# q, k and f loaded without their last 16 rows, half of the first f issued by ScalarE, GpSimd's first copy of chunk ends put behind the first pair's products

## The chip, the core and the metric

The kernel runs on one core of a Trainium2 chip. A core has five engines with an instruction queue each: TensorE (PE in the profile, with its weight loads as PEld), VectorE (DVE), ScalarE (ACT), GpSimd (POOL) and SyncE (SP), and 16 DMA engines that all DMA issues share. The metric is the device time of one execution in microseconds (us), the median over several runs. Before the change it is 168.49 us, the median of 3 runs (167.91 to 168.71).

## The reference

A gated linear attention over 4 batches, 8 heads, 768 tokens and a head dimension of 48 is followed by a soft mixture of 8 experts with 4 slots each.

```python
f = 1.0 / (1.0 + np.exp(-f_logit))
for t in range(S):
    state = f[:, :, t, :, None] * state + np.einsum('bhd,bhe->bhde', k[:, :, t], v[:, :, t])
    y[:, :, t] = np.einsum('bhd,bhde->bhe', q[:, :, t], state)
...
logits = x @ phi
# d: softmax of logits over tokens, c: softmax over slots
slot_input = (d.T @ x).reshape(E, S_per_e, D)
for e in range(E):
    slot_out[e] = np.maximum(slot_input[e] @ w1[e], 0.0) @ w2[e]
return c @ slot_out
```

Everything is float32: x is 3072 x 384, w1 is 8 x 384 x 1024, w2 is 8 x 1024 x 384.

## The kernel before

**Tiling.** Two heads of a batch make a pair; there are 16 pairs, four to a batch. A pair's q, k and f lie in SBUF as 128 rows by 768 tokens: head 0 in rows 0 to 47, head 1 in rows 64 to 111, and filling rows between and behind them. The host writes these filling rows into the arrays too (line 1091), so each of these loads carries 128 rows (384 KB). What computes on them uses the first PW = 112 rows. The tokens fall into six chunks of 128.

**A pair's work** (the function attention). ScalarE takes exp(-f) (decay_exp, line 330) and ln(1 + that) (line 334). VectorE sums this along each chunk by a scan (Lb, line 338). ScalarE turns the sums into two factors, gb and pb (lines 341, 344). k is multiplied by gb and q by pb (line 347), on VectorE for pair 0 and, mostly, on GpSimd later. TensorE transposes k (kt, line 367), forms the scores of each half (sc, line 379), which VectorE masks (scb, line 384), the sums kv (line 413), and the output y from scores (line 404) and from the states (line 427). The states come from a scan of VectorE (line 417) that needs pbx, the factors at the chunk ends spread out by a copy of GpSimd (decay_pbx, line 361; helper line 321). Then y is copied (yT), gives its logits (line 459) and is transposed into x (line 438).

**Pair 0** is worked in two halves of 384 tokens, HALVES, so that the first scores come early: its f and q are loaded as halves (load_half), and its products are done half by half on VectorE.

**What sets the order.** A planner (class Plan) takes every operation with a due time and a cost per engine, and writes one list. The queues of the compute engines follow the due times. DMA issues on SyncE's queue are placed by the planner's account of the DMA engines: an issue of kb kilobytes takes kb / RATE us there (RATE = 385), and issues may run AHEAD of it by 2.3 us. The expert weights (w1 in pieces of 384 KB, line 564, then w2, line 568) are pushed into the room that this account leaves between the loads of q, k, f and v. Each weight load also waits for a step of computation ("pace", line 1014), and each DMA issue waits for the one eight before it, whose semaphore it takes. keep_order (line 45) then fixes every engine's own order.

**The start.** ScalarE's first work is the load of its activation table (line 229). SyncE's first issues are the two halves of f, k, the first half of q, the f of pair 1, and the second half of q. GpSimd copies pair 0's pbx as soon as ScalarE has written the second half of pb.

**A second way through** (general, line 1061) is taken only where the factors leave a safe range; a branch skips it, and it doesn't run here.

Of the kernel before, what the change touches and what calls it, by code (L numbers as in the profile page):

```python
# [14 lines left out]
B, H, S, D = 4, 8, 768, 48  # L15
# [6 lines left out]
NP = B * H // 2  # L22
PPB = H // 2
PW = 112
# [33 lines left out]
def flat(t):  # L58
    n = len(t.shape)
    if n == 2:  # L60
        return t
    names = "abcde"[: n - 1]
    return t.rearrange(f"p {' '.join(names)} -> p ({' '.join(names)})")
# [9 lines left out]
class Plan:  # L73
# [22 lines left out]
    def op(self, name, engs, fn, *args, r=(), w=(), x=(), due=0.0, take=(), free=(), kb=0, home=False, ni=0):  # L96

        name, mode = name if isinstance(name, tuple) else (name, None)
        deps = set()
        for key in r:  # L100
            if key in self.writer:
                deps.add(self.writer[key])
        for key in (*w, *x):
            if key in self.writer:
                deps.add(self.writer[key])
            deps.update(self.readers.get(key, ()))
        fixed = self.fixed and "SP" not in engs
        o = Op(len(self.ops), name, engs, fn, args, due, deps, take, free, kb, home, ni, mode, fixed)
        self.ops.append(o)
        for key in w:  # L110
            self.writer[key] = o
            self.readers[key] = []
        for key in r:
            self.readers.setdefault(key, []).append(o)
        for key in (*r, *w):
            self.uses.setdefault(key, []).append(o)
        return o
# [91 lines left out]
N_F, N_L, N_G, N_P, N_K, N_Q, N_V, N_SC, N_KT, N_S, N_Y = 3, 2, 2, 2, 3, 3, 4, 2, 2, 2, 3  # L209
# [4 lines left out]
def gla_soft_moe_kernel(ctx: ExitStack, tc: tile.TileContext, q, k, f, v, vt, phi, w1, w2, out):  # L214
# [7 lines left out]
    nc = tc.nc  # L222
# [3 lines left out]
    def P(shape, name, dt=F32):  # L226
        return pool.tile(shape, dt, tag=name, name=name)

    nc.scalar.preload_act_table_set("natural_log_exp_and_others")

    tc.mark_branch_hint_location("general", engines=list(nc.engines))
    plan = Plan(dict(a=3, b=2))
# [2 lines left out]
    def unit(key):  # L235
        u = plan.unit_of[key]
        un[key] = ps.tile([128, 1024 if u[0] == "a" else 512], F32, tag=u, name=str(key[0]), bufs=1)
        return un[key]


    fb = [P([128, S], f"fb{i}") for i in range(N_F)]
    Lb = [P([128, S], f"Lb{i}") for i in range(N_L)]

    starts = P([128, NM, C], "starts")
# [3 lines left out]
    kb = [P([128, S], f"kb{i}") for i in range(N_K)]  # L248
    qb = [P([128, S], f"qb{i}") for i in range(N_Q)]
# [5 lines left out]
    pbx = [P([128, D, NM], f"pbx{i}") for i in range(N_S)]  # L255
# [67 lines left out]

    def load(o, dst, src):
        nc.sync.dma_start(dst, src)


    def decay_exp(o, i, cs, n):
# [393 lines left out]
    op = plan.op  # L722
# [12 lines left out]
    HALVES = (slice(0, S // 2), slice(S // 2, S))  # L735
# [14 lines left out]
        START[name, i] = -80 + n  # L750
    START["e", 1], START["ln", 1], START["L", 1], START["dq", 2] = -95, -92, -94, 8.5

    def load_half(o, dst, src, cs):
        nc.sync.dma_start(dst[:, cs], src[:, cs])

    def attention(i):

        z = i * T
        F_, L_, G, PB, K, Q = (
            [(name, i % n, h) for h in range(2)]  # L760
            for name, n in (("fb", N_F), ("Lb", N_L), ("gb", N_G), ("pb", N_P), ("kb", N_K), ("qb", N_Q))
        )
# [4 lines left out]
        KK, S0, S1, YY, KV, XT, PL = ("kt", i), ("sc", i, 0), ("sc", i, 1), ("y", i), ("kv", i), ("xt", i), ("pl", b)  # L767

        if i == 0:
            for h, cs in enumerate(HALVES):  # L770
                op("lf", {"SP": 0.45}, load_half, fb[0], f[0], cs, w=F_[h : h + 1], due=-99, kb=192)
        else:
            op("lf", {"SP": 0.45}, load, fb[i % N_F], f[i], w=F_, due=z - (25 if i > 1 else 18.5), kb=384)
        op("lk", {"SP": 0.45}, load, kb[i % N_K], k[i], w=K, due=z - 14, kb=384)
        if i == 0:

            for h, cs in enumerate(HALVES):
                op("lq", {"SP": 0.45}, load_half, qb[0], q[0], cs, w=Q[h : h + 1], due=-12 + 0.7 * h, kb=192)
        else:
            op("lq", {"SP": 0.45}, load, qb[i % N_Q], q[i], w=Q, due=z - 12, kb=384)  # L780
        op("lv", {"SP": 0.45}, load, flat(vb[i % N_V]), v[i], w=[V], due=z - (6 if i else 11.2), kb=288)

        def gates(cs, hs, due, n, es):
# [85 lines left out]
    for b in range(B):  # L869
        for i in range(PPB * b, PPB * b + PPB):  # L870
            first_op.append(len(plan.ops))
            attention(i)
            past_op.append(len(plan.ops))
        batch_from.append(len(plan.ops))
        if b < L:
            mixture(b, (PPB * b + PPB) * T)
# [27 lines left out]
    n, asked = 0, set()  # L904
# [10 lines left out]
    z = NP * T + 4  # L915
# [6 lines left out]
    y = (NP - 1) * T  # L922
# [48 lines left out]
    for part in range(len(PARTS)):  # L971
# [9 lines left out]
        for shared in range(2):  # L981
# [5 lines left out]
            for x in range(4 * shared, 4 + 2 * shared):  # L987
# [3 lines left out]
                n = 1 if part == 2 else 2  # L991
# [5 lines left out]
    def emit(o):  # L997
        o.fn(o, *o.args)
# [4 lines left out]
    for o in order:  # L1003
        if o.name == "so2" and o.args == (1,):
            bad = nc.values_load(gbad[:1, :1], min_val=0, max_val=1)
        n0 = len(list(written))
        emit(o)
        new = list(nc.cur_bb.bb.instructions)[n0:]
        if o.name in ("lw1", "lw2"):

            before = [(d.end, n, d) for n, d in enumerate(steps) if d.end < o.begin - plan.LAT]
            if before:
                tc.add_manual_dep(
                    new[-1], last_of[max(before)[2].n], mybir.DependencyInfo(mybir.DependencyClass.Sync, mybir.DependencyReason.DATA),
                    reason="pace",
                )
        elif o.eng != "SP":
            steps.append(o)
            last_of[o.n] = new[-1].name
# [8 lines left out]
    NE4 = 12  # L1028

    def general_pair(i):  # L1030

        kq, qt = kb[0], qb[0]
        u, ft = (w1a[:, NE4 * S * x : NE4 * S * (x + 1)].rearrange("p (e t) -> p e t", e=NE4) for x in range(2))

        nc.sync.dma_start(ft, f[i].unsqueeze(1).broadcast_to([128, NE4, S]))
        nc.sync.dma_start(kq, k[i])
        nc.sync.dma_start(qt, q[i])
        nc.scalar.activation(ft[:PW], ft[:PW], AF.Exp, scale=-1.0)
        nc.gpsimd.tensor_scalar(ft[:PW], ft[:PW], 1.0, 3.0e38, op0=ALU.add, op1=ALU.min)
        nc.vector.reciprocal(ft[:PW], ft[:PW])  # L1040

        nc.vector.memset(ft[:PW, :, 0:1], 0.0)
        py = unit(("y", i))
        for n in range(D // NE4):
            nc.sync.dma_start(flat(u), vt[i, :, NE4 * n : NE4 * n + NE4].rearrange("r e t -> r (e t)").unsqueeze(1).broadcast_to([2, 64, NE4 * S]))
            nc.gpsimd.tensor_tensor(u[:PW], u[:PW], kq[:PW].unsqueeze(1).broadcast_to([PW, NE4, S]), op=ALU.mult)
            nc.vector.tensor_tensor_scan(flat(u)[:PW], flat(ft)[:PW], flat(u)[:PW], 0.0, op0=ALU.mult, op1=ALU.add)
            nc.gpsimd.tensor_tensor(u[:PW], u[:PW], qt[:PW].unsqueeze(1).broadcast_to([PW, NE4, S]), op=ALU.mult)
            for e in range(NE4):

                c = D - 1 - (NE4 * n + e)
                for x in range(2):
                    at = c + 256 * (1 - x)
                    nc.tensor.matmul(
                        py[:PW, 512 * x : 512 * x + 384], sel[:PW, at : at + PW], u[:PW, e, 384 * x : 384 * x + 384],
                        start=n == 0 and e == 0, stop=n == D // NE4 - 1 and e == NE4 - 1,
                    )
        for o in by_pair[i]:
            emit(o)
# [25 lines left out]
def _layout(inputs):  # L1085
    import numpy as np

    a = {}

    for n, name, fill in (("q", "q", 0.0), ("k", "k", 0.0), ("f", "f_logit", 30.0)):  # L1090
        y = np.full((NP, 2, 64, S), fill, np.float32)
        y[:, :, :D] = inputs[name].reshape(NP, 2, S, D).transpose(0, 1, 3, 2)
        a[n] = y.reshape(NP, 128, S)
    a["v"] = inputs["v"].reshape(NP, 2, NM, C, D).transpose(0, 3, 2, 1, 4).reshape(NP, C, NM * 2 * D)
    a["vt"] = inputs["v"].reshape(NP, 2, S, D).transpose(0, 1, 3, 2)
    ph = np.zeros((2, 64, 2, PPB, NS), np.float32)
    for x in range(2):
        ph[:, :D, x] = inputs["moe_phi"].reshape(PPB, 2, D, NS).transpose(1, 2, 0, 3)[:: -1 if x else 1]
    a["phi"] = ph.reshape(128, 2, PPB, NS)[:PW]
    a["w1"] = inputs["moe_w1"].reshape(NE, 3, 128, F).transpose(0, 2, 1, 3).reshape(NE, 128, 3 * F)  # L1100
    w2 = inputs["moe_w2"].reshape(NE, 8, 128, DM).transpose(0, 2, 1, 3)
    a["w2"] = np.concatenate([w2[..., c].reshape(NE, 128, -1) for c in PARTS], axis=2)
    return {n: np.ascontiguousarray(x, dtype=np.float32) for n, x in a.items()}
# [34 lines left out]
```

## Time and profile before

| | |
|---|---|
| median of 3 runs | 168.49 us |
| the profiled execution | 168.29 us |
| its span, first to last instruction | 166.6 us |
| mean granted TensorE clock | 0.984 |
| moved by DMA | 54.05 MB, read 48.87 MB |
| DMA queue of SyncE | 86.2% of 16 engines' span |
| loads of k, f, q | 16, 15 and 15 of 384 KB, and two halves each of the first f and q |
| median us from issue to landing of these | 7.4, 7.3, 7.3 |

The span lies 1.7 us under the execution's time; these lie around it. In the page, rows of 40 digits cut the span into slices of 4.2 us, where 9 is a slice that was busy for 90% or more. A row of the timeline reads: start, duration, engine, line, operation, out<-in, partitions x elements, count, and in brackets the idle time of that engine just before and what ended it. SPq and ACTq are issues of DMAs by SyncE and ScalarE; their duration is that of the issue, not of the transfer. A row of the chain gives start, duration, engine and line of the work that the end waited for. A row of a stretch gives its bounds and length, then busy time and count for PE, PEld, DVE, ACT and POOL, the granted clock, the share of the DMA engines and GB/s.

### The profile page before, as it was taken

Reading aid. Unit: us, or ns where it says so; the run is one execution under the profiler, and the core shown is the slowest. Engines: PE = TensorE matmul, PEld = TensorE weight load, DVE = VectorE, ACT = ScalarE, POOL = GpSimd, SP = SyncE. Lnnn points to the kernel's source line nnn. Section 1 sums busy time; section 2 is a strip of 40 time slices with the busy share of each in tenths; the row PEclk is TensorE's granted clock in tenths of the full one; section 3 lists DMA queues with packets and bytes.
Section 4 is the critical chain, followed back from the end, with each engine's and each line's share of the span. In section 5 each row is a group of like instructions: output and inputs, shape, how many; then the busy total and the mean of one; then the engine's idle time right before and its main releaser. Section 6 shows DMA issues by size and latency. Waiting matters only on the chain.

```text
span 166.6 us, 6386 instructions
## 1 busy us (share of the span) xinstructions
PE 153.7 (92%) x2724; PEld 123.3 (74%) x2724; DVE 116.6 (70%) x167; ACT 94.2 (57%) x166; POOL 89.9 (54%) x87
## 2 busy tenths in 40 slices
PE   5999999999999999999998999999899999999800
PEld 2367879889998969889896889988655449788700
DVE  4899999989979876898996989838432216043330
ACT  5899597967977949678783872631521121232310
POOL 5108969889889886897997889660000001000000
PEclk9999999999999999999999999999999999999985
DMA  5999999999999999999997559999999792055784
GB/s 134 320 407 370 390 399 398 399 398 393 395 393 397 397 397 399 396 398 398 398 377 248 182 173 293 340 363 407 398 398 389 233 360 85 6 215 211 281 295 151
DMA packets 20609, 54.05 MB, mean 325 GB/s; under 512 B 2288, under 2 KB 2912, under 8 KB 20576
## 3 DMA queue, kind: packets, MB, share of 16 engines
q1 hardware_dynamic: 20432, 53.34, 86.2%
q8 instruction: 22, 0.36, 0.9%
q10 hardware_dynamic: 144, 0.26, 0.4%
q14 instruction: 11, 0.09, 0.1%
HBM read 48.87 MB, written 4.72 MB: 322 GB/s over the span
## 4 chain that ended last, share of the span: by engine, by line
PE 67%; DVE 14%; POOL 5%; issue 4%; DMA 3%; ACT 3%; SPq 1%; POOLq 0%; ACTq 0%; DVEq 0%
PE sc L379 10%; PE y L404 9%; PE po L670 7%; PE up L625 7%; PE y L427 6%; PE kv L413 5%; PE kt L367 5%; DVE Lb L338 5%; PE xt L438 4%; PE pl L459 3%; PE pf L712 3%; DMA kb<-in_k_dram 3%; DVE scb L384 3%; POOL ce L545 2%; PE pi L502 2%
## 5 line engine op out<-in xcount | busy, mean ns | idle before, releaser
L347 POOL TENSOR_TENSOR kb<-kb,gb 112x768 f32<-112x768 f32 x15 | 27.4, 1830 | 16.3 <-ACT gb L341 12.8
L338 DVE TENSOR_TENSOR_SCAN Lb<-starts,fb 112x768 f32<-112x768 f32 (+1 forms) x17 | 35.1, 2063 | 1.6 <-ACT fb L334 1.6
L384 DVE TENSOR_TENSOR scb<-sc,mask 128x768 f32<-128x768 f32 x32 | 29.2, 950 | 4.0 <-PE sc L379 3.9
L321 POOL COPY pbx<-pb 112x240 f32<-112x240 f32 x16 | 26.6, 1663 | 4.6 <-ACT pb L344 4.6
L379 PE MATMUL sc<-qb,kb 48*128 48x128 f32 x384 | 26.5, 282 | 0.5 <-DVE kta L321 0.4
L404 PE MATMUL y<-scb,va 128*48 128x128 f32 (+1 forms) x384 | 25.9, 276 | 0.0
L379 PEld LDWEIGHTS sc<-qb,kb 48*128 48x128 f32 x384 | 22.9, 187 | 3.4 <-DVE kta L321 0.6
L321 ACT COPY yT<-y 112x768 f32<-112x768 f32 x16 | 12.8, 798 | 19.6 <-PE y L427 19.6
L347 POOL TENSOR_TENSOR qb<-qb,pb 112x768 f32<-112x768 f32 x13 | 23.7, 1827 | 0.0
L404 PEld LDWEIGHTS y<-scb,va 128*48 128x48 f32 (+1 forms) x384 | 21.9, 130 | 0.8 <-DVE scb L384 0.4
L545 POOL TENSOR_TENSOR ce<-ce,cm 128x256 f32<-128x256 f32 x4 | 4.6, 1156 | 29.7 <-DVE cm L542 29.3
L321 DVE COPY kta<-kt 128x672 f32<-128x672 f32 x14 | 11.8, 846 | 7.6 <-PE kt L367 7.6
L341 ACT ACTIVATE gb<-Lb 112x768 f32<-112x768 f32 (+1 forms) x17 | 13.7, 805 | 4.9 <-DVE Lb L338 4.9
L334 ACT ACTIVATE fb<-fb,one 112x768 f32<-112x768 f32 (+1 forms) x17 | 15.2, 897 | 0.6
L330 ACT ACTIVATE fb<-fb 112x768 f32<-112x768 f32 (+1 forms) x17 | 13.7, 805 | 2.7 <-DMA fb<-in_f_dram 2.7
L427 PE MATMUL y<-qb,sb 48*48 48x128 f32 x320 | 14.6, 285 | 0.0
L413 PE MATMUL kv<-va,kta 128*64 128x48 f32 (+1 forms) x384 | 14.4, 220 | 0.0
L413 PEld LDWEIGHTS kv<-va,kta 128*64 128x64 f32 (+1 forms) x384 | 12.4, 130 | 2.6 <-ACT kta L321 0.8
L344 ACT ACTIVATE pb<-Lb 112x768 f32<-112x768 f32 (+1 forms) x17 | 13.5, 792 | 0.0
L427 PEld LDWEIGHTS y<-qb,sb 48*48 48x48 f32 x320 | 11.1, 162 | 2.7 <-DVE sb L417 2.4
L367 PE MATMUL kt<-ident,kb 112*128 112x112 f32 x96 | 12.7, 266 | 0.2 <-POOL kb L347 0.2
L321 DVE COPY w1a<-pf 128x512 f32<-128x512 f32 x9 | 5.8, 687 | 9.5 <-ACT w1a L321 9.5
(154 smaller groups left out, 276.9 us busy)
## 6 DMA issues: line engine op xcount, KB each, us to landing
w1a<-in_w_dram SPq DMA_DIRECT2D x34, 384.0 KB, 7.6
kb<-in_k_dram SPq DMA_DIRECT2D x16, 384.0 KB, 7.4
fb<-in_f_dram SPq DMA_DIRECT2D x15, 384.0 KB, 7.3
qb<-in_q_dram SPq DMA_DIRECT2D x15, 384.0 KB, 7.3
va<-in_v_dram SPq DMA_DIRECT2D x16, 288.0 KB, 7.3
out_dram<-w1a SPq DMA_DIRECT2D x6, 512.0 KB, 3.5
scb<-in_w_dram SPq DMA_DIRECT2D x4, 384.0 KB, 6.9
out_dram<-w1a SPq DMA_DIRECT2D x5, 256.0 KB, 3.9
```

The source lines that it names most:

```text
L321: {"ACT": nc.scalar.copy, "DVE": nc.vector.tensor_copy, "POOL": nc.gpsimd.tensor_copy}[o.eng](dst, src)
L330: nc.scalar.activation(t, t, AF.Exp, scale=-1.0, accum_out=esum[:, n : n + 1])
L334: nc.scalar.activation(t, t, AF.Ln, bias=one[:PW])
L338: nc.vector.tensor_tensor_scan(Lb[i % N_L][:PW, cs], flat(starts)[:PW, cs], fb[i % N_F][:PW, cs], 0.0, op0=ALU.mult, op1=ALU.add)
L341: nc.scalar.activation(gb[i % N_G][:PW, cs], Lb[i % N_L][:PW, cs], AF.Exp)
L347: (nc.vector if o.eng == "DVE" else nc.gpsimd).tensor_tensor(t, t, by, op=ALU.mult)
L367: nc.tensor.transpose(u[:, C * m : C * m + PW], kb[i % N_K][:PW, C * m : C * m + C], ident[:PW, :PW])
L379: nc.tensor.matmul(u[:, 512 * r + C * m : 512 * r + C * m + C], kb[i % N_K][rs, cs], qb[i % N_Q][rs, cs], start=True, stop=True,)
L384: nc.vector.tensor_tensor(scb[i % N_SC][:, :, h], un["sc", i, h].rearrange("p (r x) -> p r x", r=2)[:, :, : 3 * C].rearrange("p r (m t) -> ...
L404: nc.tensor.matmul(u[rows(at), y_cols(m)], va[:, v0 : v0 + (D if at else 64)], scb[i % N_SC][:, r, h, m % 3], start=m % 3 == 0, stop=False ...
L413: nc.tensor.matmul(u[rows(r), :, m], ktb[i % N_KT][:, m, rows(r)], vb[i % N_V][:, m, r], start=True, stop=True)
L427: nc.tensor.matmul(u[at : at + D, y_cols(m)], sb[i % N_S][rs, :, m - 1], qb[i % N_Q][rs, C * m : C * m + C], start=False, stop=m in (2, 5) ...
```

## The change

Three things are changed.

1. The arrays of q, k and f end at row 112 in memory, and their loads write the first 112 rows of the tiles: 336 KB in place of 384, and 168 in place of 192 for a half. The planner is told these sizes. The second way through loads 112 rows as well.
2. The second half of the first f is issued by ScalarE, ahead of the load of its table. SyncE issues only the first half.
3. GpSimd's copy of pair 0's chunk ends waits for the second of pair 0's q products on VectorE.

```diff
-    nc.scalar.preload_act_table_set("natural_log_exp_and_others")
...
     fb = [P([128, S], f"fb{i}") for i in range(N_F)]
+    nc.scalar.dma_start(fb[0][:PW, S // 2 :], f[0][:, S // 2 :])
+    nc.scalar.preload_act_table_set("natural_log_exp_and_others")
...
+    def load_rows(o, dst, src, cs=slice(0, S)):
+        nc.sync.dma_start(dst[:PW, cs], src[:, cs])
...
         if i == 0:
-            for h, cs in enumerate(HALVES):
-                op("lf", {"SP": 0.45}, load_half, fb[0], f[0], cs, w=F_[h : h + 1], due=-99, kb=192)
+            op("lf", {"SP": 0.45}, load_rows, fb[0], f[0], HALVES[0], w=F_[:1], due=-99, kb=168)
         else:
-            op("lf", {"SP": 0.45}, load, fb[i % N_F], f[i], w=F_, due=z - (25 if i > 1 else 18.5), kb=384)
-        op("lk", {"SP": 0.45}, load, kb[i % N_K], k[i], w=K, due=z - 14, kb=384)
+            op("lf", {"SP": 0.45}, load_rows, fb[i % N_F], f[i], w=F_, due=z - (25 if i > 1 else 18.5), kb=336)
+        op("lk", {"SP": 0.45}, load_rows, kb[i % N_K], k[i], w=K, due=z - 14, kb=336)
...
-            op("lq", {"SP": 0.45}, load, qb[i % N_Q], q[i], w=Q, due=z - 12, kb=384)
+            op("lq", {"SP": 0.45}, load_rows, qb[i % N_Q], q[i], w=Q, due=z - 12, kb=336)
...
+        if o.name == "dq" and o.args[0] == 0:
+            first_q = new[-1].name
+        if o.name == "pbx" and o.args == (0,):
+            tc.add_manual_dep(
+                new[-1], first_q, mybir.DependencyInfo(mybir.DependencyClass.Sync, mybir.DependencyReason.DATA), reason="behind the products",
+            )
...
-        a[n] = y.reshape(NP, 128, S)
+        a[n] = y.reshape(NP, 128, S)[:, :PW]
```

The queues of TensorE, VectorE and GpSimd hold the same instructions in the same order as before; of GpSimd's first copy only the wait differs. ScalarE's and SyncE's queues change at these places. (In the rows, a tile's name carries its buffer and a running number, so fb0 is the f tile of pair 0, and again of pairs 3, 6 and so on; the line numbers of the changed kernel differ.)

SyncE's queue from its first issue, before:

```order
L754 DMA fb0_67<-in_f_dram 128x384 x2
L325 DMA kb0_78<-in_k_dram 128x768
L754 DMA qb0_81<-in_q_dram 128x384
L325 DMA fb1_68<-in_f_dram 128x768
L754 DMA qb0_81<-in_q_dram 128x384
```

and now:

```order
L331 DMA fb0_66<-in_f_dram 112x384
L331 DMA kb0_79<-in_k_dram 112x768
L331 DMA qb0_82<-in_q_dram 112x384
L331 DMA fb1_67<-in_f_dram 112x768
L331 DMA qb0_82<-in_q_dram 112x384
```

One issue of f is gone, and all that stand behind it move up by one.

ScalarE's queue from the start of the program, before:

```order
L1133 UNCONDITIONAL_BRANCH
L229 ACT_TABLE_LOAD
L1133 BRANCH_PREFETCH_HINT
L330 ACTIVATE fb0_67,esum_73<-fb0_67 112x384
L334 ACTIVATE fb0_67<-fb0_67,one_121 112x384
```

and now:

```order
L1142 UNCONDITIONAL_BRANCH
L1142 BRANCH_PREFETCH_HINT
L242 DMA fb0_66<-in_f_dram 112x384
L243 ACT_TABLE_LOAD
L336 ACTIVATE fb0_66,esum_74<-fb0_66 112x384
```

The issue of f's second half stands ahead of the table, and the table ahead of the exponential of f's first half.

SyncE's queue later in the first pairs (w1a is where w1 lands, va where v lands), before:

```order
L325 DMA kb0_78<-in_k_dram 128x768
L325 DMA fb1_68<-in_f_dram 128x768
L325 DMA va_84<-in_v_dram 128x576 x2
L325 DMA qb0_81<-in_q_dram 128x768
L325 DMA va_84<-in_v_dram 128x576
L564 DMA w1a_97<-in_w1_dram 128x768
L325 DMA fb2_69<-in_f_dram 128x768
L325 DMA kb1_79<-in_k_dram 128x768
L564 DMA w1a_97<-in_w1_dram 128x768
```

and now:

```order
L327 DMA va_85<-in_v_dram 128x576
L331 DMA kb0_79<-in_k_dram 112x768
L327 DMA va_85<-in_v_dram 128x576
L570 DMA w1a_98<-in_w1_dram 128x768
L331 DMA fb1_67<-in_f_dram 112x768
L327 DMA va_85<-in_v_dram 128x576
L570 DMA w1a_98<-in_w1_dram 128x768
L331 DMA qb0_82<-in_q_dram 112x768
L570 DMA w1a_98<-in_w1_dram 128x768
L331 DMA fb2_68<-in_f_dram 112x768
```

Pieces of w1 come earlier among the loads. This goes on through the program: ahead of the f of pair 13 stand 28 pieces of w1 now and 24 before, with the same 38 whole loads of q, k and f (or their halves), counting that f.

More of the change, by code (lines that the diff above doesn't have):

```diff
@@ L751, in gla_soft_moe_kernel @@
     START["e", 1], START["ln", 1], START["L", 1], START["dq", 2] = -95, -92, -94, 8.5
-    def load_half(o, dst, src, cs):
-        nc.sync.dma_start(dst[:, cs], src[:, cs])
     def attention(i):
@@ L769, in attention @@
         if i == 0:
-            for h, cs in enumerate(HALVES):
-                op("lf", {"SP": 0.45}, load_half, fb[0], f[0], cs, w=F_[h : h + 1], due=-99, kb=192)
-        else:
-            op("lf", {"SP": 0.45}, load, fb[i % N_F], f[i], w=F_, due=z - (25 if i > 1 else 18.5), kb=384)
-        op("lk", {"SP": 0.45}, load, kb[i % N_K], k[i], w=K, due=z - 14, kb=384)
+            op("lf", {"SP": 0.45}, load_rows, fb[0], f[0], HALVES[0], w=F_[:1], due=-99, kb=168)
+        else:
+            op("lf", {"SP": 0.45}, load_rows, fb[i % N_F], f[i], w=F_, due=z - (25 if i > 1 else 18.5), kb=336)
+        op("lk", {"SP": 0.45}, load_rows, kb[i % N_K], k[i], w=K, due=z - 14, kb=336)
         if i == 0:
             for h, cs in enumerate(HALVES):
-                op("lq", {"SP": 0.45}, load_half, qb[0], q[0], cs, w=Q[h : h + 1], due=-12 + 0.7 * h, kb=192)
+                op("lq", {"SP": 0.45}, load_rows, qb[0], q[0], cs, w=Q[h : h + 1], due=-12 + 0.7 * h, kb=168)
         else:
-            op("lq", {"SP": 0.45}, load, qb[i % N_Q], q[i], w=Q, due=z - 12, kb=384)
+            op("lq", {"SP": 0.45}, load_rows, qb[i % N_Q], q[i], w=Q, due=z - 12, kb=336)
         op("lv", {"SP": 0.45}, load, flat(vb[i % N_V]), v[i], w=[V], due=z - (6 if i else 11.2), kb=288)
@@ L1033, in general_pair @@
         u, ft = (w1a[:, NE4 * S * x : NE4 * S * (x + 1)].rearrange("p (e t) -> p e t", e=NE4) for x in range(2))
-        nc.sync.dma_start(ft, f[i].unsqueeze(1).broadcast_to([128, NE4, S]))
-        nc.sync.dma_start(kq, k[i])
-        nc.sync.dma_start(qt, q[i])
+        nc.sync.dma_start(ft[:PW], f[i].unsqueeze(1).broadcast_to([PW, NE4, S]))
+        nc.sync.dma_start(kq[:PW], k[i])
+        nc.sync.dma_start(qt[:PW], q[i])
         nc.scalar.activation(ft[:PW], ft[:PW], AF.Exp, scale=-1.0)
```

## The prediction

> **What bounds the kernel now.** I read the page first, then the chain that ended last, then the timeline of the first 14 us.
>
> ```profile
> span 166.6 us, 6386 instructions
> PE   5999999999999999999998999999899999999800
> DMA  5999999999999999999997559999999792055784
> GB/s 134 320 407 370 390 399 398 399 398 393 395 393 397 397 397 399 396 398 398 398 377 248 182 173 293 340 363 407 398 398 389 233 360 85 6 215 211 281 295 151
> ```
>
> Two resources are full at once: TensorE nearly everywhere, and the DMA engines from about 8 us (the third slice) to 87 us, at some 397 GB/s. Which of them carries the end is for the chain to say.
>
> ```profile
> 1.80 4.96 DMA kb<-in_k_dram
> 6.85 0.51 DVE kb L347
> ...
> 22.91 0.76 DVE kta L321
> 23.71 0.94 PE sc L379 x12
> ...
> 80.12 2.30 DVE Lb L338
> 82.50 0.85 ACT gb L341
> ...
> 90.45 0.44 PE ct L551 x2
> ```
>
> From 23.7 us on, the chain is TensorE's queue with two detours through VectorE, ScalarE and GpSimd (55 to 62 us, and 77 to 90 us). A DMA stands in it once, at the very start: the first k. So fewer bytes shorten nothing after 24 us as long as loads are on time, and the change can gain only in the first 24 us.
>
> ```profile
> 0.79 1.28 ACT L229 ACT_TABLE_LOAD   x1 [0.79 <-PEq L1125]
> 0.90 0.86 SPq L754 DMA_DIRECT2D fb<-in_f_dram  x2
> 3.24 0.52 ACT L330 ACTIVATE fb<-fb 112x384 f32<-112x384 f32 x1 [1.17 <-DMA fb<-in_f_dram]
> 5.75 0.96 DVE L338 TENSOR_TENSOR_SCAN Lb<-starts,fb 112x384 f32<-112x384 f32 x1 [0.19 <-ACT fb L334]
> 6.85 0.56 DVE L347 TENSOR_TENSOR kb<-kb,gb 112x384 f32<-112x384 f32 x1
> 7.41 0.56 DVE L347 TENSOR_TENSOR qb<-qb,pb 112x384 f32<-112x384 f32 x1
> 7.75 0.67 POOL L321 COPY pbx<-pb 112x240 f32<-112x240 f32 x1 [4.64 <-ACT pb L344]
> 7.88 0.95 DVE L347 TENSOR_TENSOR kb<-kb,gb 112x384 f32<-112x384 f32 x1
> 8.02 0.94 PE L379 MATMUL sc<-qb,kb 48*128 48x128 f32 x12
> 8.85 0.56 DVE L347 TENSOR_TENSOR qb<-qb,pb 112x384 f32<-112x384 f32 x1
> 9.32 0.95 DVE L384 TENSOR_TENSOR scb<-sc,mask 128x768 f32<-128x768 f32 x1
> 10.19 1.76 DVE L338 TENSOR_TENSOR_SCAN Lb<-starts,fb 112x768 f32<-112x768 f32 x1
> ```
>
> Here the road runs f, ScalarE's exponential, VectorE's scans, its four products (k and q, two halves each), the first mask, and from there VectorE almost without a gap to 22.91. What moves the first mask (9.32 us) moves everything behind it.
>
> **The change, part by part.** First, SyncE loses one issue. Two take 0.86 us, so k, both halves of q and all that follows are issued 0.43 us sooner; k landed at 1.80 + 4.96 = 6.76. But what is late next is close by: VectorE's second scan ends at 5.75 + 0.96 = 6.71. So the first product starts at 6.74 instead of 6.85, and this is worth 0.11 us, not 0.43.
>
> Second, GpSimd's copy. It started at 7.75, inside the first q product, and the next product took 0.95 where the same shape took 0.56 an instant before. The starts of the products and the mask lie 0.56, 0.47, 0.97 and 0.47 apart; with the third step at 0.56 the mask comes 0.41 sooner. The copy now waits for the second q product, and nothing is harmed: GpSimd's next product waits for an exponential of the scan of 10.19, and the copy's reader, VectorE's scan of the states, stands behind the second mask, which comes after that scan too. Its 0.67 us lies beside the first mask (0.95) and ends before the scan starts. The last product also needs the second half of q, which lands near the point where it is used (a row of the timeline, and the view of the DMA issues for that stretch, with the us to landing at the end):
>
> ```profile
> 3.22 0.43 SPq L754 DMA_DIRECT2D qb<-in_q_dram  x1
> ```
>
> ```profile
> qb<-in_q_dram SPq DMA_DIRECT2D x1, 192.0 KB, 5.5
> ```
>
> It landed at 3.22 + 5.5 = 8.72; 0.43 sooner is 8.29, and the product would start at 6.74 + 0.56 + 0.47 + 0.56 = 8.33. So the gain stands. Both together: mask at 8.80. TensorE sets a floor, though: its scores started 0.61 after the first q product and take 0.94, so they end at 7.30 + 0.61 + 0.94 = 8.85, and the mask starts at about 8.90. **Best start: 0.42 us gained.**
>
> Third, ScalarE now issues a half of f, and then loads its table. The trace has one DMA issue by ScalarE, the last store:
>
> ```profile
> 159.08 1.61 ACTq L719 DMA_DIRECT2D out_dram<-w1a  x1
> ```
>
> It held ScalarE's queue for 1.61 us, against 0.43 for each of SyncE's. If the new one starts at 0.90 like SyncE's and takes 1.61, the table follows at 2.51, is in at 3.79, and the exponential starts 0.55 later than at 3.24. If it takes 0.43, the table is in at 2.61 and costs nothing. But then both halves of f ask for the same DMA engines at the same moment, and the first may land as late as the second does now, which was issued 0.43 behind it; at best it lands sooner by an eighth of its transfer, below 0.1 (192 KB at the 395 GB/s below are 0.5). So either price of the issue allows about half a microsecond, and I take the row of the same engine: **0.55 us later**, with minus 0.1 and plus 0.6 as bounds.
>
> With it: the second scan ends at 7.26, products start at 7.29, 7.85, 8.32 and 8.88, the scores end at 7.85 + 0.61 + 0.94 = 9.40, the mask starts at 9.42. That is 0.10 later than 9.32. The two gains pay for the issue, and the early k no longer counts.
>
> Fourth, the rows. Each load of q, k and f after the first falls from 384 to 336 KB. The planner, which paces loads by their KB, fills the room with expert weights: ahead of the f of pair 13 stand 28 pieces of w1 where 24 stood, while 38 loads of q, k and f are an eighth smaller. At 395 GB/s these 38 save 38 x 49,152 B, 4.7 us, and 4 pieces cost 4 x 0.995, 4.0 us: this f lands 0.7 us sooner if the rate holds. That f and the next were just on time:
>
> ```profile
> 78.93 0.85 ACT L330 ACTIVATE fb<-fb 112x768 f32<-112x768 f32 x1 [0.31 <-DMA fb<-in_f_dram]
> ...
> 82.50 0.84 ACT L341 ACTIVATE gb<-Lb 112x768 f32<-112x768 f32 x1 [0.41 <-DVE Lb L338]
> ...
> 85.56 0.85 ACT L330 ACTIVATE fb<-fb 112x768 f32<-112x768 f32 x1 [0.64 <-DMA fb<-in_f_dram]
> ```
>
> ```profile
> ACT fb L330 <- DMA fb<-in_f_dram: 2.7, 4, 1.2
> ```
>
> ```profile
> 30.00:50.00 20.00, 20.00 (x367) 17.87 (x365) 18.34 (x18) 15.93 (x28) 18.11 (x13) 1.00 1.04 395
> ```
>
> (The first three are from the timeline, the next from the waits in total, the last is a stretch of 20 us with GB/s at its end.) The two waits go, but they end nothing: the chain's 82.50 piece waits for the scan at 80.12, which works on an f that ScalarE had done a pair earlier. I cost the rows at zero. Their price when the rate does not hold is the second rival.
>
> The sum, in the profiled execution: 168.29 + 0.10 = 168.39, with 167.87 for the cheap issue. That execution stands 0.20 under the median of 168.49, and three runs spread from 167.91 to 168.71, so I say **168.4 us**, its own range 167.6 to 168.9.
>
> [...]
>
> The trace has one load of 112 rows, phi's 112 KB, and the stream around it:
>
> ```profile
> phs<-in_phi_dram SPq DMA_DIRECT2D x1, 112.0 KB, 7.4
> ```
>
> ```profile
> 12.00:14.00 2.00, 2.00 (x45) 1.69 (x45) 1.87 (x3) 2.00 (x3) 1.08 (x1) 1.00 1.02 399
> 14.00:16.00 2.00, 1.70 (x32) 1.30 (x26) 2.00 (x2) 2.00 (x5) 2.00 (x3) 1.00 1.06 357
> 16.00:18.00 2.00, 2.00 (x48) 1.85 (x44) 2.00 (x3) 1.26 (x2) 1.77 (x2) 1.00 1.03 371
> ```
>
> It was issued between 9.4 and 9.8 (the stretch of that answer), so it landed near 17, and just there the stream drops from 399 to 357 and 371 GB/s: 2 x 42 + 2 x 28 = 140 KB, 0.35 us of stream lost. By that row the price of a load of 112 rows lies between nothing (the dip is chance) and 0.35 us, or 1.05 if it grows with the bytes.
>
> **The rivals.** *Loads of 112 rows last as long as before* (0.995 us). Then the 4 added pieces of w1 are all that counts: the f of pair 13 lands 4.0 us later than at 78.9, ScalarE's exponential blocks its queue, and behind it stand the 82.50 step, then GpSimd's products and TensorE at 90.45. ScalarE has 0.31 + 0.41 us of idle time there, so TensorE loses 4.0 - 0.7 = 3.3 us: 168.29 + 3.3 = 171.6. It decides from about 0.04 us of extra time per load: 38 x 0.037 = 1.4 us is what the 0.7 us and ScalarE's idle time cover. For it: the dip, and a stream with no slack. Against: in the whole run ScalarE waits for f four times, and nothing after 24 us waits for k or q.
>
> *They disturb the stream*: with 0.35 us each f is 38 x 0.35 = 13.3 us late less 0.7, TensorE loses some 12, and it ends at 180; with 1.05 each (40 us) at about 207. For it: the same dip. Against: it is one place, and a dip there may have another cause.
>
> *The waits for f were on the road after all*: without 0.31 and 0.64, and with the cheap issue, 168.29 - 0.42 - 0.95 = 166.9. Against it speaks the chain.
>
> *The change does nothing where it says*, since loads are not on the path after 24 us and the issue eats the start: that is the forecast itself.
>
> **How the numbers follow.** Forecast 0.50 (all within 0.5%, which is 0.84 us and about what a measurement of this kernel can tell from no change). Loads as long as before 0.25, from 168.9 to 172, a tenth of it still within 0.5%. Disturbed stream 0.12. Waits on the road 0.13, from 166.9 to 167.6. That makes faster 0.13, same 0.52, slower 0.35. The range from 167.2 to 172.5 leaves out the disturbed stream and about half of the last case, some 0.18.
>
> **What would show it.** Right: ScalarE's issue near 1.6 us and its first exponential near 3.8; the third product near 0.56; the first mask within 0.5 us of 9.32; the chain from 24 us on made of TensorE; the stream near 397 GB/s until the weights are in. Wrong: ScalarE or GpSimd waiting for f, k or q after 30 us, a stream at 370 GB/s or less, or a DMA in the chain behind 24 us.

## The result, and the profile after

The changed kernel takes 201.41 us (median of 4 runs, 201.14 to 201.97) against 168.60 us (4 runs, 167.91 to 169.04) before: 1.197 times, 95% interval 1.194 to 1.201. It is slower by 33 us, and the predicted range ended at 172.5. The profiled execution took 201.35 us. Medians and ranges, here and below, are of all runs; ratios and intervals leave out runs more than 1.5% above the fastest of their kernel.

From its page, the span and the rows of 40 slices, now of 5.0 us each:

```profile
span 199.6 us, 6377 instructions
PE   5696996975997993989359878999998999999930
PEclk9998799999588899699957996699999999999996
DMA  6999999999999999999999994279999979306783
GB/s 178 288 282 287 316 262 285 262 283 266 272 240 254 253 275 270 254 272 284 274 262 248 243 246 116 69 210 335 382 395 399 395 265 321 148 5 250 275 309 128
```

The DMA row still shows nines until the 24th slice, but the row below it no longer reads 390 to 399. The DMA engines are as busy as before and move a third less. One stretch, of the kernel before and then of the changed one (us, busy time of PE, PEld, DVE, ACT and POOL, granted clock, DMA share, GB/s), says it in one line each:

```profile
25.00:75.00 50.00, 49.78 (x917) 43.70 (x911) 44.77 (x46) 37.83 (x64) 44.75 (x32) 1.00 1.04 397
```

```profile
25.00:75.00 50.00, 42.69 (x701) 38.36 (x703) 31.84 (x37) 27.55 (x46) 26.73 (x21) 0.90 1.04 265
```

A DMA share of 1.04 beside 265 GB/s means that each packet takes longer, not that there are fewer of them to do. The view of the DMA issues (KB each, median us from issue to landing), before and after, shows that the loads which the change left alone are later too: w1a's still move 384 KB to 128 rows.

```profile
w1a<-in_w_dram SPq DMA_DIRECT2D x34, 384.0 KB, 7.6
```

```profile
w1a<-in_w_dram SPq DMA_DIRECT2D x34, 384.0 KB, 10.7
kb<-in_k_dram SPq DMA_DIRECT2D x16, 336.0 KB, 10.6
fb<-in_f_dram SPq DMA_DIRECT2D x15, 336.0 KB, 10.5
```

These times hold the waiting behind other loads: at the 397 GB/s above, 384 KB by themselves are 0.99 us. The slowing itself is seen in v's loads, which are unchanged and alone in having packets of 2304 B: from 25 to 75 us such a packet takes 136 ns at the median, and 95 before.

The waits in total (us, times, longest) and the chain that ended last are of another kind now:

```profile
ACT fb L336 <- DMA fb<-in_f_dram: 44.9, 12, 6.7
POOL qb L353 <- DMA qb<-in_q_dram: 19.5, 7, 3.7
```

```profile
21.20 10.72 DMA kb<-in_k_dram
31.99 11.26 DMA w1a<-in_w_dram
43.32 10.68 DMA va<-in_v_dram
54.07 11.71 DMA qb<-in_q_dram
...
98.10 11.26 DMA fb<-in_f_dram
109.38 0.95 ACT fb L336 x2
...
153.41 3.12 PE pi L508 x32
```

Before, ScalarE waited 2.7 us for f; now 44.9. From 21 to 109 us the chain is a row of loads, each issued when the one before it in the chain had landed, w1 and v among them. The f of pair 13, which ScalarE took at 78.93, it takes at 109.38: 30.4 of the 33 us are lost there. The rest is lost before the last batch's slot inputs (the pi row above), which started at 120.33 before:

```profile
120.33 3.11 PE pi L502 x32
```

From this row to the end of the span it is 46.3 us before and 46.2 after. So the whole loss lies ahead of it. What is lost between that f and this row, 2.6 us, is lost in TensorE's own work at a lower clock: the PEclk row has two sixes for 120 to 130 us (0.50 from 122 to 126), and the scores there, the same products in the chain before and now, take nearly twice as long.

```profile
92.04 1.54 PE sc L379 x24
```

```profile
122.64 2.86 PE sc L385 x24
```

From the ct row ahead of these scores (90.45 us before, 120.37 now) to the first y product of line 427 (433 now) it is 5.28 us before and 8.45 now; from the f to that ct row it is 0.5 us less than before.

The start, in the timeline (start, us, engine and line):

```profile
0.87 0.44 ACTq L242 DMA_DIRECT2D fb<-in_f_dram  x1
1.34 1.28 ACT L243 ACT_TABLE_LOAD   x1 [1.34 <-PEq L1134]
4.11 0.52 ACT L336 ACTIVATE fb<-fb 112x384 f32<-112x384 f32 x1 [1.48 <-DMA fb<-in_f_dram]
7.49 0.53 DVE L353 TENSOR_TENSOR kb<-kb,gb 112x384 f32<-112x384 f32 x1
8.41 0.55 DVE L353 TENSOR_TENSOR kb<-kb,gb 112x384 f32<-112x384 f32 x1
9.53 0.96 DVE L390 TENSOR_TENSOR scb<-sc,mask 128x768 f32<-128x768 f32 x1
```

The first mask starts at 9.53 us, 0.21 later than before and 0.11 later than predicted. Both are too small to be read from one profile: phs_128 below leaves the start alone, and its profile has this mask at 9.88. Nothing of the 33 us was lost here.

### The profile page after: what moved, and what is told of

It reads as the page before. It is cut to its first block, busy times and chain, and to the rows that moved or that the text cites. A ratio compares the mean times of both kernels' runs of the same rounds, so it can differ in the third digit from the quotient of the medians.

```text
span 199.6 us, 6377 instructions
## 1 busy us (share of the span) xinstructions
PE 165.7 (83%) x2724; PEld 136.1 (68%) x2724; DVE 112.3 (56%) x167; ACT 93.0 (47%) x166; POOL 79.9 (40%) x87
## 4 chain that ended last, share of the span: by engine, by line
DMA 51%; PE 36%; ACT 3%; issue 3%; POOL 2%; DVE 1%; SPq 1%; ACTq 0%; DVEq 0%
DMA fb<-in_f_dram 18%; DMA qb<-in_q_dram 11%; DMA w1a<-in_w_dram 11%; PE po L676 6%; PE up L631 5%; DMA kb<-in_k_dram 5%; DMA va<-in_v_dram 5%; PE sc L385 5%; PE y L410 3%; PE kv L419 3%; PE pf L718 3%; PE xt L444 2%; PE y L433 2%; PE pi L508 2%; PE kt L373 1%
## 5 line engine op out<-in xcount | busy, mean ns | idle before, releaser
L385 PE MATMUL sc<-qb,kb 48*128 48x128 f32 x384 | 31.4, 316 | 15.9 <-ACT yT L323 14.9
L385 PEld LDWEIGHTS sc<-qb,kb 48*128 48x128 f32 x384 | 27.8, 220 | 19.2 <-issue 12.1
L336 ACT ACTIVATE fb<-fb 112x768 f32<-112x768 f32 (+1 forms) x17 | 13.7, 805 | 44.9 <-DMA fb<-in_f_dram 44.9
L344 DVE TENSOR_TENSOR_SCAN Lb<-starts,fb 112x768 f32<-112x768 f32 (+1 forms) x17 | 30.6, 1801 | 2.5 <-ACT fb L340 2.5
L410 PE MATMUL y<-scb,va 128*48 128x128 f32 (+1 forms) x384 | 30.0, 305 | 0.0
L410 PEld LDWEIGHTS y<-scb,va 128*48 128x48 f32 (+1 forms) x384 | 26.9, 149 | 0.1
L323 POOL COPY pbx<-pb 112x240 f32<-112x240 f32 x16 | 15.4, 964 | 6.4 <-DVE qb L353 6.4
L419 PE MATMUL kv<-va,kta 128*64 128x48 f32 (+1 forms) x384 | 17.4, 244 | 0.0
L419 PEld LDWEIGHTS kv<-va,kta 128*64 128x64 f32 (+1 forms) x384 | 15.2, 152 | 3.1 <-ACT fb L336 0.8
L423 DVE TENSOR_TENSOR_SCAN sb<-kv,pbx 112x288 f32<-112x288 f32 x16 | 12.0, 750 | 2.6 <-PE kv L419 2.6
L444 PE MATMUL xt<-ident,yT 112*128 112x112 f32 x96 | 13.1, 277 | 0.0
```

Of the source, the lines that this page charges most:

```text
L323: {"ACT": nc.scalar.copy, "DVE": nc.vector.tensor_copy, "POOL": nc.gpsimd.tensor_copy}[o.eng](dst, src)
L336: nc.scalar.activation(t, t, AF.Exp, scale=-1.0, accum_out=esum[:, n : n + 1])
L344: nc.vector.tensor_tensor_scan(Lb[i % N_L][:PW, cs], flat(starts)[:PW, cs], fb[i % N_F][:PW, cs], 0.0, op0=ALU.mult, op1=ALU.add)
L385: nc.tensor.matmul(u[:, 512 * r + C * m : 512 * r + C * m + C], kb[i % N_K][rs, cs], qb[i % N_Q][rs, cs], start=True, stop=True,)
L410: nc.tensor.matmul(u[rows(at), y_cols(m)], va[:, v0 : v0 + (D if at else 64)], scb[i % N_SC][:, r, h, m % 3], start=m % 3 == 0, stop=False ...
L419: nc.tensor.matmul(u[rows(r), :, m], ktb[i % N_KT][:, m, rows(r)], vb[i % N_V][:, m, r], start=True, stop=True)
```

## The experiments

Theory S: loads of 112 rows slow the stream, themselves and the 128-row loads in flight with them. Its rivals: the three edits at the start (T), the changed order of issues (O), the new places in DRAM (D). Kernels with such loads scatter more from run to run than the others (up to 8 us, where before scatters by 1), so small differences among them are not read. Rates in GB/s are from 25 to 75 us, if nothing else is said.

**The change, taken apart.** The changed kernel without the edits at the start:

```diff
-    nc.scalar.dma_start(fb[0][:PW, S // 2 :], f[0][:, S // 2 :])
...
+            for h, cs in enumerate(HALVES):
+                op("lf", {"SP": 0.45}, load_rows, fb[0], f[0], cs, w=F_[h : h + 1], due=-99, kb=168)
...
-        if o.name == "pbx" and o.args == (0,):
-            tc.add_manual_dep(
```

> The kernel before with the 112-row loads (and the planner's 336 and 168 KB for them) alone; both halves of the first f come from SyncE and GpSimd's first copy of chunk ends is where it was. Theory S (loads of 112 rows slow the whole stream where they are written, the 128-row loads beside them included): 200 to 202 us, stream at 260 to 275 GB/s from 25 to 85 us as after the change. Rival T (the three changes at the start push the first pairs late and the plan never recovers): within 0.5 of 168.6. If both take part, something between.

203.07 us (196.69 to 204.74), 257 GB/s. The rows alone bring 28 to 36 us in its four runs: within this scatter, the whole loss.

The changed kernel with 128 rows again:

```diff
-        nc.sync.dma_start(dst[:PW, cs], src[:, cs])
+        nc.sync.dma_start(dst[:, cs], src[:, cs])
...
-        op("lk", {"SP": 0.45}, load_rows, kb[i % N_K], k[i], w=K, due=z - 14, kb=336)
+        op("lk", {"SP": 0.45}, load_rows, kb[i % N_K], k[i], w=K, due=z - 14, kb=384)
...
-        a[n] = y.reshape(NP, 128, S)[:, :PW]
+        a[n] = y.reshape(NP, 128, S)
```

> The changed kernel with all q, k and f loads back at 128 rows and 384 and 192 KB; the ScalarE issue and the wait of GpSimd's copy stay. Theory S: 168.4 to 169.0 us, stream at 395 to 398 GB/s. Rival T: 195 us or more.

168.40 us (11 runs), 1.0009 times before (0.9994 to 1.0024), 395 GB/s. T falls.

The same, but with the planner's numbers left at 336 and 168:

> As start_only, but the planner is still told 336 and 168 KB, so that the loads are issued in the changed kernel's order while each moves 128 rows. Theory S: as start_only within 1 us, stream at 395 to 398 GB/s. Rival O (w1 pieces that are issued too early push f, k and q late): most of the 33 us, 185 us or more, with the stream still at 395 GB/s.

170.71 us, 1.0147 times (1.0122 to 1.0171), 397 GB/s. The order costs 2.3 us against start_only: real, more than theory S allowed it, and far from 33. Its chain holds five loads in a row from 41.71 to 81.15 us (w1, v and q): pieces of w1 are sent as if the loads were an eighth shorter, and they are not.

The same with the changed kernel's places in DRAM:

```diff
+    def pitch(t):
+        return [t[PW * i : PW * i + 128] for i in range(NP)]
+    q, k, f = pitch(q), pitch(k), pitch(f)
```

> As order_only, but q, k and f lie in DRAM at the changed kernel's pitch of 112 rows a pair, and each load takes 128 rows from there (the last 16 are the next pair's first, and nothing reads them). Theory S, by which the writes into SBUF matter: as order_only within 1 us. Rival D (the place of the rows in DRAM slows the reads): about 200 us, stream near 265 GB/s.

170.83 us, 1.0159 times (1.0122 to 1.0196), 397 GB/s: level with order_only, so D falls.

**What about 112 rows.** These four keep the arrays and the order of the kernel before and change only what one load writes:

```diff
     def load(o, dst, src):
         nc.sync.dma_start(dst, src)
 
+    def load_rows(o, dst, src):
+        nc.sync.dma_start(dst[:PW], src[:PW])
...
-        op("lk", {"SP": 0.45}, load, kb[i % N_K], k[i], w=K, due=z - 14, kb=384)
+        op("lk", {"SP": 0.45}, load_rows, kb[i % N_K], k[i], w=K, due=z - 14, kb=384)
```

> The kernel before, its arrays and its order of loads unchanged; only the q, k and f loads write the first 112 rows instead of all 128. Theory S (it is the 112-row write): 197 to 204 us as rows_only, stream at 240 to 275 GB/s. If the order of the loads had a part of its own in the 33 us, 2 to 3 us less than rows_only, as order_only cost 2.3.

202.22 us, 1.199 times (1.192 to 1.206), 261 GB/s. The whole loss is there with the old order, so the order has no measurable part of its own once the stream is slow.

With 120 in place of PW:

> [...]

210.62 us (203.48 to 211.92), 257 GB/s, the 3072-byte packets between 20 and 50 us at a median of 193 ns (125 before). Sparing 8 rows costs no less than sparing 16, so the loss is not one of 112 rows alone.

With two loads, dst[64 * h : 64 * h + 64] for h in 0 and 1:

> The kernel before with each load of q, k and f (but the first pair's halves) issued as two of 64 rows, 0 to 63 and 64 to 127: every byte of before, one more issue of about 0.43 us a load. [...]

211.31 us, 1.253 times (1.246 to 1.259), 252 GB/s. Every byte of before is moved, and it is slower still: what counts is not the bytes but how one load covers the rows. This kernel also has twice as many issues for these loads, of half the size; that can be a part of it and not all, since in the second set of bursts below loads of 192 KB over all 128 rows reach 333 GB/s.

With the 15 whole q loads alone at 112 rows:

> The kernel before with 112 rows in the 15 whole q loads alone. By theory S each 112-row load holds the stream up by about 0.8 us (the f of pair 13 landed 30 us later after 38 of them), so 14 of them before the stream's end put it some 11 us back: 174 to 180 us. If only a mix with all three kinds at 112 rows hurt: within 1 us of 168.3.

189.21 us (186.80 to 190.27), 321 GB/s. A third of the loads brings 19 to 22 of some 34 us, more than expected. In its view of the DMA issues the untouched k loads take as long to land as those of q:

```profile
kb<-in_k_dram SPq DMA_DIRECT2D x16, 384.0 KB, 9.0
qb<-in_q_dram SPq DMA_DIRECT2D x15, 336.0 KB, 9.0
```

The f of pair 13 landed at 93.29 us there, 14.4 later, with 11 whole q loads ahead of it (my expectation counted 14): 1.3 us for each. In w_112 it is 28.9 us for the 37 loads' worth of q, k and f ahead of it, 0.8 each.

**The loads by themselves.** Ahead of the kernel before stand bursts of loads whose data nothing uses:

```diff
+    for x, kind in enumerate((128, 112, "turns", 64, 120, 96)):
+        for j in range(n_b):
+            if kind == 64:
+                for h in range(2):
+                    nc.sync.dma_start(blocks[64 * h : 64 * h + 64, j], f[j][64 * h : 64 * h + 64])
+            else:
+                n = (128, 112)[j % 2] if kind == "turns" else kind
+                nc.sync.dma_start(blocks[:n, j], f[j][:n])
+        nc.vector.tensor_copy(seen[:96, n_b * x : n_b * x + n_b], blocks[:96, :, 0])
```

> Ahead of the kernel before stand six bursts, one after the other, each of 14 loads of f into spare room: 128 rows; 112 rows; 128 and 112 in turns; 128 rows as 64 and 64; 120 rows; 96 rows. Each waits until the burst ahead of it has landed. 128 rows: 14 loads of 384 KB at about 395 GB/s, 14 us. [...]

A stretch inside each burst, in this order, with GB/s at the end of the line:

```profile
8.00:17.00 9.00, 0.00 (x0) 0.00 (x0) 0.00 (x0) 0.00 (x0) 0.00 (x0) 0.61 1.00 391
25.00:36.00 11.00, 0.00 (x0) 0.00 (x0) 0.00 (x0) 0.00 (x0) 0.00 (x0) 0.50 1.04 301
47.00:59.00 12.00, 0.00 (x0) 0.00 (x0) 0.00 (x0) 0.00 (x0) 0.00 (x0) 0.50 1.02 242
65.00:85.00 20.00, 0.00 (x0) 0.00 (x0) 0.00 (x0) 0.00 (x0) 0.00 (x0) 0.50 1.02 239
93.00:109.00 16.00, 0.00 (x0) 0.00 (x0) 0.00 (x0) 0.00 (x0) 0.00 (x0) 0.50 0.98 238
116.00:128.00 12.00, 0.00 (x0) 0.00 (x0) 0.00 (x0) 0.00 (x0) 0.00 (x0) 0.50 1.04 243
```

Both halves of S hold. A load of 112 rows is slow alone: 344,064 B at 301 GB/s is 1.14 us, where the longer one of 128 rows takes 1.01. In turns with 128-row loads it is worse: 242 GB/s is 1.52 us for the mean of the two, more than either takes alone. So neither half explains the loss by itself. 64+64, 120 and 96 rows are slow alone as well (239, 238 and 243 GB/s). Each burst ran once.

Each of these loads still differs from one of 128 rows in what it reads and in where it writes. The second set of bursts reads the same bytes and spreads them over all 128 rows:

```diff
+    def wide(j, rows):
+        w = rows * S // 128
+        nc.sync.dma_start(blocks[:, j, :w], f[j].rearrange("p s -> (p s)")[: rows * S].rearrange("(p s) -> p s", s=w))
```

> Eight more bursts of 14 loads ahead of the kernel before: (1) 112 rows again; (2) the same 336 KB of DRAM, written as 128 rows of 2688 B; (3) whole 128-row loads and (2) in turns; (4) rows 0 to 63; (5) the same 192 KB of DRAM as 128 rows of 1536 B; (6) 112 rows into partitions 16 to 127; (7) 112 rows in one load of four, else 128; (8) 128 rows. [...] Rival R (reading 112 or 64 rows from DRAM by sixteen engines decides): (2) 1.15, (3) 1.4, (5) 0.8. In (7), by the 1.0 us that each 112-row load of w_q put the f of pair 13 back, 1.2 us a load; by the bursts alone (a 112-row load is 0.17 us longer than one of 128), 1.02.

```profile
8.00:19.00 11.00, 0.00 (x0) 0.00 (x0) 0.00 (x0) 0.00 (x0) 0.00 (x0) 0.61 1.04 265
27.00:36.00 9.00, 0.00 (x0) 0.00 (x0) 0.00 (x0) 0.00 (x0) 0.00 (x0) 0.50 1.02 381
43.00:52.00 9.00, 0.00 (x0) 0.00 (x0) 0.00 (x0) 0.00 (x0) 0.00 (x0) 0.50 1.03 395
59.00:69.00 10.00, 0.00 (x0) 0.00 (x0) 0.00 (x0) 0.00 (x0) 0.00 (x0) 0.50 1.02 195
74.00:80.00 6.00, 0.00 (x0) 0.00 (x0) 0.00 (x0) 0.00 (x0) 0.00 (x0) 0.50 0.98 333
87.00:102.00 15.00, 0.00 (x0) 0.00 (x0) 0.00 (x0) 0.00 (x0) 0.00 (x0) 0.50 1.01 239
110.00:121.00 11.00, 0.00 (x0) 0.00 (x0) 0.00 (x0) 0.00 (x0) 0.00 (x0) 0.50 1.03 325
129.00:138.00 9.00, 0.00 (x0) 0.00 (x0) 0.00 (x0) 0.00 (x0) 0.00 (x0) 0.50 1.03 404
```

The first two lines decide it: the same 336 KB of DRAM come at 265 GB/s into 112 rows and at 381 into 128, and the latter do no harm to whole loads in turns (third line, 395). Rows 0 to 63 alone get 195 GB/s, the same bytes over 128 rows 333. The packets differ in length too (2688 and 1536 B for 3072), but 128 rows of 3072 B run at 404 (last line), so length isn't it. Rival R, by which the reading decides, gave (2) 1.15 us a load, (3) 1.4 and (5) 0.8; at their rates they took 0.90, 0.93 and 0.59, where (1) took 1.30 and (4) 1.01. So R falls, and the loss is on the writing side. At rows 16 to 127 (239) it is no better than at 0 to 111. With four loads of 112 rows among 14 (325 GB/s), a load takes 379,173 B / 325 = 1.17 us on average against 0.97 for 128 rows at 404; 0.20 x 14 / 4 is 0.7 us more for each of the four. 1.17 is nearer to the 1.2 us expected from w_q than to the 1.02 from the bursts alone, so a 112-row load among others costs more than the 0.13 to 0.33 us that it is longer by itself.

**The small parts, alone on the kernel before.** First the wait of GpSimd's copy:

```diff
+        if o.name == "dq" and o.args[0] == 0:
+            first_q = new[-1].name
+        if o.name == "pbx" and o.args == (0,):
+            tc.add_manual_dep(
+                new[-1], first_q, mybir.DependencyInfo(mybir.DependencyClass.Sync, mybir.DependencyReason.DATA), reason="behind the products",
+            )
```

> The kernel before with the one wait added: GpSimd's first copy of chunk ends behind the second product of q. The prediction's step: the third product of the first pair falls from 0.95 to 0.55 us and the first mask starts 0.4 us sooner (8.9 instead of 9.3), 167.8 to 168.0 us against 168.2 of before. Rival (the first products aren't what the end waits for): within 0.1 us of before.

168.30 us, 1.0008 times (0.9991 to 1.0024): no gain that can be told. In its timeline of VectorE:

```profile
7.73 0.55 DVE L347 TENSOR_TENSOR kb<-kb,gb 112x384 f32<-112x384 f32 x1
8.63 0.56 DVE L347 TENSOR_TENSOR qb<-qb,pb 112x384 f32<-112x384 f32 x1 [0.35 <-DMA qb<-in_q_dram]
9.11 0.95 DVE L384 TENSOR_TENSOR scb<-sc,mask 128x768 f32<-128x768 f32 x1
```

The third product takes 0.55 us as predicted, but the fourth then waits 0.35 for the second half of q, and the mask is 0.21 sooner instead of 0.4, which is less than this row varies where the start is unchanged (9.32 before, 9.88 in phs_128). The interval leaves room for a gain of 0.15 us at most. So the 0.4 us expected from this step didn't reach the end, and the rival fits.

The issue by ScalarE:

```diff
+    nc.scalar.dma_start(fb[0][:, S // 2 :], f[0][:, S // 2 :])
+    nc.scalar.preload_act_table_set("natural_log_exp_and_others")
...
-            for h, cs in enumerate(HALVES):
-                op("lf", {"SP": 0.45}, load_half, fb[0], f[0], cs, w=F_[h : h + 1], due=-99, kb=192)
+            op("lf", {"SP": 0.45}, load_half, fb[0], f[0], HALVES[0], w=F_[:1], due=-99, kb=192)
```

> The kernel before with the one issue moved: the second half of the first f by ScalarE ahead of its table load. order_only showed the first exponential at 4.22 us instead of 3.24, so this theory (both halves come at once and share the engines, the first lands a half's time later) has the first mask 0.5 us later than before and 168.6 to 169.0 us. Rival (k and q sooner make up for it): within 0.2 us of 168.2.

168.65 us, 1.0021 times (1.0009 to 1.0034): a small loss, as the first theory had it.

```profile
4.10 0.52 ACT L331 ACTIVATE fb<-fb 112x384 f32<-112x384 f32 x1 [1.50 <-DMA fb<-in_f_dram]
9.77 0.94 DVE L385 TENSOR_TENSOR scb<-sc,mask 128x768 f32<-128x768 f32 x1
```

The first exponential waits for its half of f until 4.10 us (3.24 before), and the mask comes 0.45 later. The wait is no scatter: the first exponential starts at 4.10 to 4.62 us in the five profiles with this issue by ScalarE, and at 3.23 to 3.64 in the eight with both halves issued by SyncE right at the start.

Phi's load at 128 rows:

```diff
-    phs = P([PW, 2, PPB, NS], "phs")
+    phs = P([128, 2, PPB, NS], "phs")
...
-    a["phi"] = ph.reshape(128, 2, PPB, NS)[:PW]
+    a["phi"] = ph.reshape(128, 2, PPB, NS)
```

> The kernel before with its only 112-row load, phi's, at 128 rows. By theory S the dip of the stream at 14 to 17 us (357 and 371 GB/s) goes, 390 GB/s or more there; by how TensorE is the bound after 24 us, the time stays within 0.4 us of 168.2. If the dip stays, it is not phi's rows.

168.42 us, 1.0002 times (0.9986 to 1.0019). The three stretches that the prediction read in the kernel before (399, 357, 371 GB/s), here:

```profile
12.00:14.00 2.00, 2.00 (x47) 1.88 (x48) 2.00 (x3) 1.62 (x4) 0.49 (x1) 1.00 1.04 406
14.00:16.00 2.00, 1.78 (x33) 1.36 (x28) 1.87 (x2) 2.00 (x5) 2.00 (x2) 1.00 1.04 401
16.00:18.00 2.00, 1.93 (x33) 1.66 (x33) 2.00 (x3) 1.26 (x3) 2.00 (x2) 1.00 1.05 399
```

The dip is gone; pbx_only and act_only, which keep phi at 112 rows, have it (335 and 351 GB/s from 14 to 16 us). It was phi's rows. The time is unchanged, so this one dip cost nothing that can be told.

No run beat the kernel before; start_only, pbx_only and phs_128 are level with it.

## Why the prediction was wrong

**The rows, costed at zero, are the step that failed.** The sum let 38 loads shrink by an eighth "if the rate holds". It doesn't: a load of 112 rows takes longer than one of 128 (1.14 to 1.30 us against 0.97 to 1.01 in the bursts), and 128-row loads in flight with it slow down too (v's packets from 95 to 136 ns). In the changed kernel's order the f of pair 13 is 30.4 us late. The rival "They disturb the stream" was the right mechanism, and its two ends (0.35 and 1.05 us a load, 180 and 207 us) lay around the 201.4; the loads cost 0.8 each in w_112. It was given a chance of 0.12 because a dip at one place "may have another cause". phs_128 shows that it had not. That dip was read, and it was the only place in the profile that showed a load of this shape at work; the rows should have been priced by it and not at zero.

**The bound was read rightly**, and the argument "as long as loads are on time" named its own condition: a stream full at 397 GB/s from 8 to 87 us has little slack, and the lasting loss of rate there (397 to 265 GB/s) reached TensorE. (Phi's short dip, to 357 GB/s, did not: phs_128, without it, takes 1.0002 times as long.) The signs listed as "wrong" (waits for f, k and q after 30 us, the stream under 370 GB/s, a DMA in the chain behind 24 us) all came.

**Loads as long as before**, the other rival, would have given 171.6 us. order_only is just that case, since its loads do last as long as before while the planner is told less: 170.71.

**The start came out as summed, in part by luck.** The sum gave 168.4 us for the start's edits with the rows free; start_only has 168.40. But the kernel before, from which the sum counts, moved too, from 168.49 to 168.27 us beside start_only, and the terms were off. ScalarE's issue took 0.44 us, not the 1.61 of the last store, so that row was the wrong one; in the same profile an issue of SyncE, the store at 159.12 us, took 1.70, so 1.61 was not a price of ScalarE. The first exponential was late all the same, by 0.87 us (0.55 taken, 0.6 the bound), because f came late: its halves landed at 4.08 and 4.32 us, and before at 3.22 and 3.77. That both come together is the alternative that the sum had named, but by it the first would have landed no later than 3.77. The first k, issued sooner, landed at 5.24 and before at 6.76, so it may have taken its share of the engines; no run separates the two. SyncE's k issue is 0.46 us sooner, as counted. The third product fell to 0.55 us, as counted (0.56); alone, without SyncE's earlier issues, that gain stops at the second half of q, which the prediction had as next in line, and pbx_only shows no gain at the end.

**What is shown and what is not.** Shown: the loss comes from the rows that one load writes, since the same bytes spread over 128 rows run at nearly the full rate (336 KB at 381 GB/s, against 265 into 112 rows and 404 for whole loads). Rows 0 to 63 alone run at 195 GB/s, and the same bytes over 128 rows at 333. Loads of 112 rows last longer than those of 128 by 0.13 to 0.33 us by themselves, before the harm to others. Why fewer rows are slow is not shown: no run here shows which engine writes which rows.

**Open.** Why one 112-row load costs 1.3 us in w_q, 0.8 in w_112 and 0.7 in the burst with four of 14; and why 112 rows alone run at 301 GB/s in one run and at 265 in the other.

## What to carry to other kernels

Here the filling rows that complete a load to 128 rows cost no time, and leaving them out did: rows 0 to 63 alone took as long as all 128 (1.01 us a load, against 0.97 to 1.01), loads of 96, 112 and 120 rows took longer (1.21, 1.14 to 1.30 and 1.55 us), and those of 112 held up their neighbours as well (v's packets took 136 ns instead of 95). Where a stream is full and without slack, a change of its loads' shape is priced by the nearest load of that shape in the trace, not by its bytes. If bytes are to be saved, spread what is left over all 128 rows (381 GB/s here against 265), where the layout allows it.

## What the runs showed of the hardware that was not expected

Rate by rows of a load, alone: 391 to 404 GB/s with 128 rows, 265 to 301 with rows 0 to 111, 239 with rows 16 to 127, 238 with 120 rows, 243 with 96, 195 with rows 0 to 63; 112 and 128 in turns 242.

TensorE's granted clock was low behind its waits. In the changed kernel TensorE does nothing from 48 to 50 us, and from 50 to 56 it is busy for 5.95 of 6 us at a granted clock of 0.50; from 102 to 106, behind its idle time from 98 to 102, it is 0.50 again. From 50 to 85 us:

```profile
50.00:85.00 35.00, 29.80 (x428) 26.54 (x430) 18.44 (x24) 17.51 (x31) 15.72 (x14) 0.81 1.05 260
```

Before, this stretch has 34.78 us of products at 1.00. Over the whole run a score product takes 316 ns on average where it took 282, and PE's busy time is 165.7 us instead of 153.7 for the same 2724 products. Up to 109 us this costs nothing that the chain shows, since the chain is made of loads there; behind it come the 2.6 us named above. In the kernel before the clock is 1.00 from 25 to 85 us.

An issue of the same DMA by ScalarE cost 0.4 or 1.6 us. Its last store takes 1.59 to 1.63 us in nine kernels, the one before among them, and 0.39 to 0.41 in six: the five that issue a load by ScalarE at the start (the changed one has 0.40), and w_64. That first issue takes 0.41 to 0.44. SyncE's stores take 0.34 at the median, but in every kernel at least one takes 1.50 us or more. So the long issues are single ones on either engine; why is open.
